# The first pass's SiLU written as h*(1+tanh(h/2))/2 in a fused attention and two-layer kernel

## The chip, the cores and the metric

One core of one Trainium2 chip runs the whole program in one launch. The metric is device time in microseconds. The kernel before took 858.95 us, the median of three runs (857.21 to 859.91).

## The reference

A linear attention with softmax over features (q) and over the sequence (k), then two feed-forward layers. The kernel's inputs are drawn so that q is spread by 0.8 and k by about 0.46; the weights are float64.

```
q_s = softmax(q, axis=-1);  k_s = softmax(k, axis=2)
kv  = einsum('bhsd,bhse->bhde', k_s, v);  x = einsum('bhsd,bhde->bhse', q_s, kv)
x   = x.transpose(0, 2, 1, 3).reshape(2304, 512)
h = x @ w_in1;  g = h * (1 / (1 + exp(-h)));      x = g @ w_out1     # SiLU, 512 -> 2048 -> 512
h = x @ w_in2;  g = h * tanh(log(1 + exp(h)));    out = g @ w_out2   # Mish, 512 -> 2048 -> 512
```

## The kernel before, in words

Every float32 product is made of three products of a reduced float32 type: an operand is split into a rounded high part and the rest, and high*high, high*low and low*high are added in the accumulator. So a step `x @ w` of 128 rows of w and 384 tokens takes three TensorE products.

The first layer runs in two passes over the hidden dimension, 8 of its 16 chunks of 128 each. The first pass (p = 0) goes through six blocks of 384 tokens, the second (p = 1) through five mostly 512 wide. For a block and chunk c, `ev_g1` makes h (12 products into one accumulator bank, 4 or 5 in turn), then SiLU, the rounded high part `g[:, 0]` and the rest `g[:, 1]`; `ev_g2` multiplies g into four accumulators (banks 0 to 3, 12 products), three chunks later (`SKEW = 3`, line 94). So at the start of a block four G1 stand in a row, and the third needs the bank of the first. At a block's end `ev_e` copies the four accumulators out, in the first pass with a plain copy, two on ScalarE and two on VectorE.

The first pass is interleaved with two other streams. The attention of the later blocks (`attn_steps`: k transposed with TensorE, its largest value on VectorE, Exp on ScalarE, back by TensorE and a ScalarE copy, the product with v, then q) works in banks 6 and 7, in the same queues. And in block 0 each weight tile is decoded from float64 just before its use (`w_decode`): on ScalarE one Prelu and one rounding copy, on VectorE a shift (`st`), a join (`wt`) and a subtraction (`wall`), 16 tiles in all.

Until the last part of the first pass the order of an engine's instructions is the choice of a scheduler: the program gives priorities (`at`) and the scheduler weighs them with its own idea of durations. From then on (`InOrder.on`) each engine's order is that of the code. In the profile an instruction of the scheduled part has line 57, one of the ordered part (and of the first attention block) line 59: the two calls of the recording helper. Once built, each engine works through its list in order, and an instruction that waits holds up all behind it.

The lines that matter: 712 takes the bank of h, 723 is SiLU from that bank, 724 the rounding (VectorE in the first pass, ScalarE in the second), 725 the subtraction, 747 and 749 the copies out of the accumulators. Where names follow, `gf` is the activation's result, `g` its two parts, `xs` the tokens, `knm` the largest value of k negated, `kz` its sum, `qmx` the largest value of q.

Of the kernel before, what the change touches and what calls it, by code (L numbers as in the profile page):

```python
# [10 lines left out]
ACTF = mybir.ActivationFunctionType  # L11
ALU = mybir.AluOpType
# [53 lines left out]
def attention_silu_mish(ctx: ExitStack, tc: tile.TileContext, q, k, v, w_in1, w_out1, w_in2, w_out2, out):  # L66
    nc = tc.nc
    V, S, G, T, SP = (InOrder(tc, e) for e in (nc.vector, nc.scalar, nc.gpsimd, nc.tensor, nc.sync))
# [69 lines left out]
    def banks(name, ids, n=1):  # L138
        i = turns[name] = (turns.get(name, -1) + 1) % len(ids)
        return psum[:, ids[i] * 512:(ids[i] + n) * 512]  # L140
# [99 lines left out]
    def w_get(kind, p, c):  # L240
        while p == 0 and (kind, p, c) not in wt:
            w_decode()
        return wt[(kind, p, c)]
# [465 lines left out]
    def ev_g1(p, j, c):  # L709
        w = w_get("G1", p, c)  # L710
        x = xs[(p, j)]
        h = banks("h1", (4, 5))[:, :blocks[p][j][1]]

        steps = [(kc, i) for i in range(3) for kc in range(KC)]
        if (p, j) == (0, 0) and c < 2:
            steps.sort()
        for n, (kc, i) in enumerate(steps):
            s = slice(kc * P, (kc + 1) * P)
            T.matmul(h, w[:, i // 2, s], x[:, kc, i % 2], start=(n == 0), stop=(n == len(steps) - 1))
        n = blocks[p][j][1]  # L720
        g = pools["g"].tile([P, 2, n], F32R, tag="g", name="g")
        gf = pools["gf"].tile([P, n], F32, tag="gf", name="gf")
        S.activation(out=gf, in_=h, func=ACTF.Silu)
        (S.copy if p else V.tensor_copy)(g[:, 0], gf)
        V.tensor_tensor(out=g[:, 1], in0=gf, in1=g[:, 0].bitcast(F32), op=ALU.subtract)
        gt[(p, j, c)] = g

# [12 lines left out]
    def ev_e(p, j):  # L740
        t0, n = blocks[p][j]
        for i, a in enumerate(acc[(p, j)]):
            y = xbT[:, i, t0:t0 + n]
            if p:
                V.tensor_tensor(out=y, in0=a[:, :n], in1=y, op=ALU.add)
            elif i % 2:
                V.tensor_copy(y, a[:, :n])
            else:
                S.copy(y, a[:, :n])

# [117 lines left out]
    def more():  # L870

        o_split()
        if not wait:
            return
        s, c, b = wait.pop(0)
        if s is None:
            ev_g2(1, len(WIDE) - 1, c)
            if c == NCH - 1:
                ev_e(1, len(WIDE) - 1)
            o_load(c - HALF - 3)  # L880
            return
        for n in range(BLK // P):
            second(s, c, b, n)
        if done[(s, b, 0)] == NCH:
            for n in range(BLK // P):
                out_tile(s, b, n)
        k = used[(s, c)] = used.get((s, c), 0) + 1
        if k == 2:
            o_load(s * NCH + c + O_RING)
# [3 lines left out]
    def pair(s, q):  # L893
# [64 lines left out]
        out=ident, in_=ident, compare_op=ALU.not_equal, fill=1.0, base=0, pattern=[[-1, P]], channel_multiplier=1  # L958
# [35 lines left out]
    for i, (what, p, j, c) in enumerate(events):  # L994
# [26 lines left out]
        if what == "E":  # L1021
            at(i if InOrder.on else i - X_LEAD)
            ev_e(p, j)
            continue
        (ev_g1 if what == "G1" else ev_g2)(p, j, c)
        if (what, p, j) == ("G1", 1, len(WIDE) - 1):
            n = c - HALF
# [72 lines left out]
```

## Time and the profile before

| | |
|---|---|
| median of three runs | 858.95 us |
| lowest and highest run | 857.21 and 859.91 us |
| span of the profiled execution, first to last instruction | 856.9 us |
| TensorE busy | 843.4 us, 98% |
| VectorE, ScalarE, GpSimd busy | 466.4, 365.3, 55.0 us |
| granted TensorE clock | 1.000 of full speed |

The profile lists no separate time of its execution beside the span; the median of the runs stands 2.05 us over that span. PE is TensorE's products and PEld its weight loads, which overlap; DVE is VectorE, ACT ScalarE, POOL GpSimd, SP the engine that issues DMAs. Busy times of neighbours on one engine overlap by some hundredths of a us, so what an instruction takes from its engine is the distance from its start to the next start.

### The profile page before, as it was taken

How to read it: one execution, taken by the hardware profiler on the slowest of the kernel's cores; microseconds unless marked ns; L12 is line 12 of the kernel's file. 1: busy time of each engine (PE TensorE's matmuls, PEld its weight loads, DVE VectorE, ACT ScalarE, POOL GpSimd, SP SyncE). 2: the span in 40 equal slices, each digit the busy share in tenths (PEclk: the TensorE clock that was granted, in tenths of full speed). 3: DMA queues.
4: the chain of work that ended last, by engine and by line, in shares of the span. 5: the costliest groups of instructions: out<-in, count | busy, mean ns of one | idle time of the engine just before them, and what ended most of it. 6: DMA issues, size and time to landing. Idle time of an engine off the chain costs nothing.

```text
span 856.9 us, 12318 instructions
## 1 busy us (share of the span) xinstructions
PE 843.4 (98%) x4666; PEld 755.6 (88%) x4666; DVE 466.4 (54%) x1004; ACT 365.3 (43%) x702; POOL 55.0 (6%) x82
## 2 busy tenths in 40 slices
PE   8899999999999999999999999999999999999998
PEld 7688988899999888898888899998999998999996
DVE  5998466673256656556574656675343554343431
ACT  5987254564244644335434444444322233322221
POOL 3145111221000000000000000000000000000000
PEclk9999999999999999999999999999999999999999
DMA  9996311220023438675633778888555455664312
GB/s 237 233 257 132 90 37 37 55 57 1 1 78 120 148 99 283 209 251 178 210 117 106 272 260 314 294 321 340 211 182 223 161 196 184 233 225 155 135 50 98
DMA packets 86105, 145.49 MB, mean 170 GB/s; under 512 B 33056, under 2 KB 60192, under 8 KB 82976
## 3 DMA queue, kind: packets, MB, share of 16 engines
q1 hardware_dynamic: 86048, 144.73, 52.2%
q8 instruction: 36, 0.59, 0.3%
q14 instruction: 21, 0.17, 0.1%
HBM read 105.38 MB, written 39.32 MB: 169 GB/s over the span
## 4 chain that ended last, share of the span: by engine, by line
PE 90%; DVE 3%; ACT 3%; DMA 2%; SPq 1%; issue 1%; ACTq 0%; DVEq 0%
PE psum L59 70%; PE psum L57 19%; DMA st<-in_moe_w_in_dram 2%; SPq L57 1%; ACT xa L57 1%; ACT wt L57 0%; DVE g L57 0%; DVE wt L59 0%; DVE kmx L57 0%; DVE wall L57 0%; DVE xs L59 0%; DVE wt L57 0%; ACT xs L59 0%; ACT L57 0%; ACT wall L57 0%
## 5 line engine op out<-in xcount | busy, mean ns | idle before, releaser
L59 PE MATMUL psum<-wall,g 128*128 128x512 f32 x864 | 210.1, 390 | 0.0
L59 PE MATMUL psum<-x,wall 128*128 128x384 f32 x1008 | 191.8, 338 | 0.0
L59 PEld LDWEIGHTS psum<-wall,g 128*128 128x128 f32 x864 | 161.3, 188 | 28.5 <-DVE xb L59 0.3
L59 PEld LDWEIGHTS psum<-x,wall 128*128 128x128 f32 x1008 | 179.9, 187 | 6.8
L59 PE MATMUL psum<-g,wall 128*128 128x512 f32 (+2 forms) x624 | 129.0, 360 | 0.0
L59 PE MATMUL psum<-xs,wall 128*128 128x512 f32 (+2 forms) x588 | 122.7, 362 | 0.2 <-ACT gf L59 0.2
L59 PEld LDWEIGHTS psum<-g,wall 128*128 128x128 f32 x624 | 109.0, 188 | 14.7
L59 PEld LDWEIGHTS psum<-xs,wall 128*128 128x128 f32 x588 | 102.7, 188 | 15.5 <-ACT gf L59 0.6
L59 DVE TENSOR_TENSOR hf<-psum,sc 128x384 f32<-128x384 f32 x72 | 40.0, 556 | 123.4 <-ACT sc L59 79.1
L57 PE MATMUL psum<-xs,wall 128*128 128x384 f32 x468 | 98.2, 349 | 3.2 <-ACT gf L57 2.3
L59 ACT COPY sc<-psum 128x384 f32<-128x384 f32 x72 | 34.5, 479 | 133.0 <-PE psum L59 133.0
L57 PEld LDWEIGHTS psum<-xs,wall 128*128 128x128 f32 x468 | 80.4, 189 | 7.5 <-ACT gf L57 3.6
L57 PE MATMUL psum<-g,wall 128*128 128x384 f32 x432 | 85.3, 343 | 0.5 <-DVE g L57 0.5
L57 PEld LDWEIGHTS psum<-g,wall 128*128 128x128 f32 x432 | 74.7, 188 | 2.1 <-DVE g L57 1.2
L59 ACT ACTIVATE hf<-hf 128x384 f32<-128x384 f32 x72 | 37.8, 525 | 84.9 <-DVE hf L59 84.8
L59 DVE TENSOR_TENSOR g<-gf,g 128x512 fp32r<-128x512 f32 (+2 forms) x49 | 30.5, 623 | 74.7 <-ACT g L59 74.4
L59 ACT ACTIVATE gf<-psum 128x512 f32<-128x512 f32 (+2 forms) x49 | 26.6, 543 | 98.6 <-PE psum L59 97.8
L59 DVE CAST g<-hf 128x384 fp32r<-128x384 f32 x96 | 34.5, 360 | 58.1 <-ACT hf L59 57.7
L59 DVE TENSOR_TENSOR g<-hf,g 128x384 fp32r<-128x384 f32 x96 | 53.6, 559 | 3.3
L59 ACT ACTIVATE wt<-st 128x512 f32<-128x512 f32 x48 | 32.0, 674 | 19.0 <-DMA st<-in_moe_w_out_dram 8.5
L57 DVE CAST g<-gf 128x384 fp32r<-128x384 f32 x39 | 16.1, 414 | 38.9 <-ACT gf L57 38.8
L57 ACT ACTIVATE gf<-psum 128x384 f32<-128x384 f32 x39 | 18.9, 491 | 40.9 <-PE psum L57 37.6
(123 smaller groups left out, 748.0 us busy)
## 6 DMA issues: line engine op xcount, KB each, us to landing
wall<-wq SPq DMA_DIRECT2D x16, 1792.0 KB, 7.5
st<-in_moe_w_in_dram SPq DMA_DIRECT2D x32, 512.0 KB, 4.8
st<-in_moe_w_out_dram SPq DMA_DIRECT2D x32, 512.0 KB, 4.4
wall<-wo SPq DMA_DIRECT2D x32, 512.0 KB, 3.6
wq<-wall SPq DMA_DIRECT2D x8, 1792.0 KB, 6.2
wo<-wall SPq DMA_DIRECT2D x16, 512.0 KB, 5.6
wqf<-wt SPq DMA_DIRECT2D x24, 256.0 KB, 3.3
wall<-wqf SPq DMA_DIRECT2D x24, 256.0 KB, 6.5
```

The costliest lines, as they stand in the source:

```text
L57: return call(*args, **kwargs)
L59: self.last = call(*args, **kwargs)
```

## The change

In the first pass SiLU becomes two instructions. ScalarE makes tanh(h/2) from the bank into `gf`; VectorE makes (gf + 1) * h, reading `gf` and the bank. The rounding copy goes from VectorE to ScalarE. What comes out is twice SiLU, and the half is put into the copy out of the accumulators. The second pass keeps Silu and its ScalarE rounding.

```
         gf = pools["gf"].tile([P, n], F32, tag="gf", name="gf")
-        S.activation(out=gf, in_=h, func=ACTF.Silu)
-        (S.copy if p else V.tensor_copy)(g[:, 0], gf)
+        if p:
+            S.activation(out=gf, in_=h, func=ACTF.Silu)
+        else:
+
+            S.activation(out=gf, in_=h, func=ACTF.Tanh, scale=0.5)
+            V.scalar_tensor_tensor(out=gf, in0=gf, scalar=1.0, in1=h, op0=ALU.add, op1=ALU.mult)
+        S.copy(g[:, 0], gf)
         V.tensor_tensor(out=g[:, 1], in0=gf, in1=g[:, 0].bitcast(F32), op=ALU.subtract)
...
             elif i % 2:
-                V.tensor_copy(y, a[:, :n])
+                V.tensor_scalar(out=y, in0=a[:, :n], scalar1=0.5, scalar2=None, op0=ALU.mult)
             else:
-                S.copy(y, a[:, :n])
+                S.mul(y, a[:, :n], 0.5)
```

The scheduler sees other instructions and makes another order on every engine. Three places in block 0 follow. ScalarE first, from the Prelu of the seventh weight tile; before, where `gf` is Silu's result and `kz` marks an Exp:

```order
L57 ACTIVATE wt_758<-st_709 128x512
L57 ACT_TABLE_LOAD
L57 ACTIVATE gf_429<-psum_126 128x384
L57 CAST wall_72<-wt_640 128x512
L57 CAST wall_72<-wt_703 128x512
L57 CAST wall_72<-wt_758 128x512
L57 ACTIVATE wt_818<-st_764 128x512
L57 ACTIVATE gf_506<-psum_126 128x384
L57 CAST wall_72<-wt_818 128x512
L57 ACT_TABLE_LOAD
L57 ACTIVATE xb_125,kz_459<-psum_126,knm_457 128x576
```

And now:

```order
L57 ACTIVATE wt_763<-st_713 128x512
L57 ACTIVATE gf_429<-psum_126 128x384
L57 ACTIVATE gf_507<-psum_126 128x384
L57 CAST wall_72<-wt_644 128x512
L57 CAST wall_72<-wt_707 128x512
L57 ACTIVATE wt_823<-st_769 128x512
L57 CAST wall_72<-wt_763 128x512
L57 CAST wall_72<-wt_823 128x512
L57 ACTIVATE xb_125,kz_460<-psum_126,knm_458 128x576
```

The table loads are gone here; in the whole program 23 of them become 3. Both chunks' activations now stand ahead of the roundings of the weights.

VectorE at the same place. Before, from the join of the seventh weight tile:

```order
L57 SCALAR_TENSOR_TENSOR wt_758<-wt_758,st_709 128x512
L57 CAST g_428<-gf_429 128x384
L57 TENSOR_TENSOR wall_72<-wt_640,wall_72 128x512
L57 TENSOR_TENSOR wall_72<-wt_703,wall_72 128x512
L57 TENSOR_TENSOR wall_72<-wt_758,wall_72 128x512
L57 SCALAR_TENSOR_TENSOR wt_818<-wt_818,st_764 128x512
L57 TENSOR_REDUCE knm_457<-psum_126 128x1
```

And now, from the shift of the eighth tile (`st_769`) to the join of the ninth (`wt_890`):

```order
L57 TENSOR_SCALAR st_769<-st_769 128x512
L57 TENSOR_TENSOR wall_72<-wt_644,wall_72 128x512
L57 TENSOR_TENSOR wall_72<-wt_707,wall_72 128x512
L57 SCALAR_TENSOR_TENSOR wt_763<-wt_763,st_713 128x512
L57 SCALAR_TENSOR_TENSOR wt_823<-wt_823,st_769 128x512
L57 TENSOR_REDUCE knm_458<-psum_126 128x1
...
L57 TENSOR_REDUCE qmx_468<-xb_125 96x4
L57 TENSOR_SCALAR st_829<-st_829 128x512
L57 SCALAR_TENSOR_TENSOR gf_429<-gf_429,psum_126 128x384
L57 SCALAR_TENSOR_TENSOR wt_890<-wt_890,st_829 128x512
L57 SCALAR_TENSOR_TENSOR gf_507<-gf_507,psum_126 128x384
L57 TENSOR_TENSOR g_428<-gf_429,g_428 128x384
```

What is left out there: two more subtractions of weights (`wall`), `kz`, the other `qmx` and the reciprocal `krz`, five rows in all. The multiplication that frees the first chunk's bank stands behind all of it.

TensorE, from the last four products of chunk 0's G1 on. Before:

```order
L57 MATMUL psum<-xs,wall 128x384 x19
L57 MATMUL psum<-ident,xa 128x96 x6
L57 MATMUL psum<-xs,wall 128x384 x21
L57 MATMUL psum<-g,wall 128x384 x8
L57 MATMUL psum<-ident,xa 128x96 x6
L57 MATMUL psum<-g,wall 128x384 x7
L57 MATMUL psum<-xs,wall 128x384 x12
L57 MATMUL psum<-g,wall 128x384
L57 MATMUL psum<-ident,xb 96x128 x6
L57 MATMUL psum<-g,wall 128x384 x10
L57 MATMUL psum<-xb,xa 64x64 x12
```

And now:

```order
L57 MATMUL psum<-xs,wall 128x384 x16
L57 MATMUL psum<-ident,xa 128x96 x6
L57 MATMUL psum<-xs,wall 128x384 x2
L57 MATMUL psum<-ident,xa 128x96 x6
L57 MATMUL psum<-xs,wall 128x384 x7
L57 MATMUL psum<-ident,xb 96x128 x6
L57 MATMUL psum<-xs,wall 128x384 x7
L57 MATMUL psum<-xb,xa 64x64 x12
L57 MATMUL psum<-xs,wall 128x384 x8
L57 MATMUL psum<-g,wall 128x384 x12
```

Ahead of these rows both lists have 8 of the 384-wide products on `xs`. `ident,xa` transposes k of a pair of heads, `ident,xb` takes its Exp back, and `xb,xa 64x64` is that pair's product with v. Before the first such product with v, G1 of chunk 4 and 26 products on `g` stood; now it stands amid G1 of chunk 3, with no product on `g` ahead of it.

## Rows read from the trace of the kernel before

**Rows 1.** The page, part 1: busy us, share of the span, instructions.

```profile
PE 843.4 (98%) x4666; PEld 755.6 (88%) x4666; DVE 466.4 (54%) x1004; ACT 365.3 (43%) x702; POOL 55.0 (6%) x82
```

**Rows 2.** Stretches: length, busy time by engine, clock, DMA share, GB/s.

```profile
20.00:60.00 40.00, 35.65 (x269) 29.19 (x270) 38.01 (x88) 36.27 (x66) 11.49 (x13) 1.00 1.03 251
60.00:90.00 30.00, 29.60 (x214) 26.50 (x214) 25.93 (x66) 23.09 (x46) 14.70 (x19) 1.00 0.80 160
90.00:250.00 160.00, 158.96 (x1049) 148.30 (x1048) 81.89 (x202) 70.65 (x132) 21.91 (x33) 1.00 0.12 31
250.00:800.00 550.00, 549.83 (x2751) 490.50 (x2750) 294.29 (x591) 213.63 (x419) 0.00 (x0) 1.00 0.61 212
```

**Rows 3.** Groups by line and shape: busy us, mean ns of one, idle before.

```profile
L57 ACT ACT_TABLE_LOAD x22 | 28.2, 1283 | 4.0 <-PE psum L57 2.3 <-PEq L1084 0.7 <-DVE knm L57 0.6
...
L57 ACT ACTIVATE gf<-psum 128x384 f32<-128x384 f32 x39 | 18.9, 491 | 40.9 <-PE psum L57 37.6 <-DVE g L57 1.6 <-issue 1.6
...
L59 DVE TENSOR_TENSOR hf<-psum,sc 128x384 f32<-128x384 f32 x72 | 40.0, 556 | 123.4 <-ACT sc L59 79.1 <-PE psum L59 44.4
...
L57 DVE TENSOR_TENSOR g<-gf,g 128x384 fp32r<-128x384 f32 x39 | 24.5, 628 | 0.9
...
L57 DVE CAST g<-gf 128x384 fp32r<-128x384 f32 x39 | 16.1, 414 | 38.9 <-ACT gf L57 38.8
...
L57 ACT CAST xs<-xa 128x384 fp32r<-128x384 f32 x16 | 7.4, 511 | 4.6 <-PE psum L57 4.4
...
L57 DVE COPY xb<-psum 128x384 f32<-128x384 f32 x8 | 4.1, 552 | 7.5 <-PE psum L57 7.5
...
L57 ACT COPY xb<-psum 128x384 f32<-128x384 f32 x8 | 3.4, 481 | 10.1 <-PE psum L57 10.1
```

**Rows 4.** TensorE in order of time: start, us, what, idle before and releaser.

```profile
33.83 0.79 PE L57 MATMUL psum<-xs,wall 128*128 128x384 f32 x3 [1.41 <-ACT gf L57]
...
40.59 0.98 PE L57 MATMUL psum<-g,wall 128*128 128x384 f32 x4 [0.49 <-DVE g L57]
...
48.19 0.92 PE L57 MATMUL psum<-xb,xa 96*64 96x64 f32 x24
...
52.11 1.68 PE L57 MATMUL psum<-xs,wall 128*128 128x384 f32 x8 [0.89 <-ACT gf L57]
...
91.44 2.24 PE L57 MATMUL psum<-g,wall 128*128 128x384 f32 x12
93.52 2.24 PE L57 MATMUL psum<-xs,wall 128*128 128x384 f32 x12
```

**Rows 5.** VectorE in order of time, 34 to 40 us.

```profile
34.00 0.43 DVE L57 TENSOR_SCALAR st<-st 128x512 uint32<-128x512 uint32 x1 [0.85 <-DMA st<-in_moe_w_in_dram]
34.34 0.68 DVE L57 SCALAR_TENSOR_TENSOR wt<-wt,st 128x512 uint32<-128x512 uint32 x1
...
35.21 1.89 DVE L57 TENSOR_TENSOR wall<-wt,wall 128x512 fp32r<-128x512 f32 x3
...
37.62 0.75 DVE L57 TENSOR_REDUCE knm<-psum 128x1 f32<-128x576 f32 x1
...
39.00 0.74 DVE L57 TENSOR_REDUCE qmx<-xb 96x4 f32<-96x256 f32 x2
```

**Rows 6.** ScalarE in order of time, 31 to 48 us.

```profile
31.99 1.28 ACT L57 ACT_TABLE_LOAD   x1
33.28 0.49 ACT L57 ACTIVATE gf<-psum 128x384 f32<-128x384 f32 x1
...
39.67 0.74 ACT L57 ACTIVATE xb<-psum,knm 128x576 f32<-128x576 f32 x1
40.31 0.19 ACT L57 ACTIVATION_READ_ACCUMULATOR xb<-psum,knm 128x1 f32 x1
...
45.99 1.34 ACT L57 ACTIVATE xb<-xb 96x256 f32<-96x256 f32 x4
47.23 0.79 ACT L57 COPY xa<-psum 96x768 f32<-96x768 f32 x1
```

## The prediction, on record before the changed kernel ran

> **What bounds the kernel now.** I read the page's engine shares first: TensorE is busy for 843.4 of 856.9 us [rows 1], so a change can save at most what TensorE still idles, and every new idle us of TensorE is paid in full unless an old one goes with it. Then the stretches [rows 2], to see where it idles: 4.35 us from 20 to 60 us (40.00 less 35.65), 0.40 from 60 to 90, 1.04 from 90 to 250, and 0.17 in the 550 us after that. The first pass begins within the first stretch, and there VectorE (38.01 of 40 us) and ScalarE (36.27) are nearly full as well, with the decoding of 16 weight tiles, the attention and the first chunks. Last the order of time in that stretch. The reader is to see that two of TensorE's gaps end with ScalarE's SiLU: 1.41 us before 33.83 and 0.89 us before 52.11 [rows 4]. In front of the first stands a table load of 1.28 us [rows 6].
>
> **What the change removes.** ScalarE has 22 table loads in the scheduled part at 1283 ns [rows 3]; 23 become 3 in the whole program, since Exp and Tanh no longer alternate with another table. That is 20 x 1.283 = 25.7 us of ScalarE. It is worth to the end only what TensorE waits for, the two gaps: 2.30 us. All others lie beside a busy TensorE.
>
> The Trainium skill ("ScalarE: Activation LUTs", section on table sets) puts exp and tanh into one set, asks to batch activations by set, and counts about 2.66 us for a switch with a drain. Here the activation starts 1.29 us after its load does [rows 6], so I see the load and no drain; the page would make it 53 us of ScalarE where the rows make it 25.7. Neither is time at the end by itself; what it could free is the first rival below.
>
> **What it adds.** Per chunk, 48 times: on ScalarE a rounding of 0.51 us (a 128x384 rounding, nearest row `xs`), 24.5 us in all, so ScalarE's sum hardly changes. On VectorE a multiplication in place of a rounding of 0.41. The trace shows no 384-wide multiplication of this form; the nearest are the addition of a bank and a tile, 0.556, and the subtraction of `g`, 0.628 [rows 3]. I take 0.56, reading a bank and a tile as this does, and keep 0.63. That is +0.15 to +0.21 us a chunk, 7 to 10 us of VectorE beside a busy TensorE, except where VectorE decides. The scaled copies out stand for 0.55 and 0.48 us [rows 3] and I leave them at that: an activation from a bank of this size takes 0.49, so twelve on ScalarE could cost 0.01 each, and they lie three chunks ahead of the next use of their banks.
>
> **What it moves: the bank.** Before, h's bank was free when ScalarE had read it. Now it is free when VectorE has multiplied. In steady running G1 of chunk c+2 starts three groups of 12 products after G1 of chunk c, that is 3 x 2.08 = 6.2 us (12 products start 2.08 us apart [rows 4], 0.1733 each), and activation and multiplication take 0.49 + 0.56 and two handovers: no stop. At a block's start four G1 stand in a row and 2.08 us are left for the same 1.05 and handovers: still enough if VectorE is free. In block 0 it is not free, and the new order shows it.
>
> **The stop, step by step.** The activations of chunks 0 and 1 come early, about 32 and 32.5 us, as no load stands before them. But VectorE's list has the multiplication of chunk 0 behind thirteen instructions, of which the first is the shift at 34.00. That one waits for its DMA [rows 5], as it will again. From there, start to start: shift 0.34; two weight subtractions and two joins at 0.60 (the three subtractions of rows 5 take 1.89), 2.40; largest of k 0.67; two more subtractions 1.20; `kz`, `qmx`, `krz`, `qmx` 0.10 + 0.33 + 0.10 + 0.33 (two `qmx` take 0.74); shift 0.34. Sum 5.81, so the multiplication starts at 39.81 and ends at 40.37. Does anything on the way wait longer? The Exp that `kz` waits for starts when `knm` ends, about 37.5, and takes 0.74 + 0.19 [rows 6]: 38.4, while `kz` is due at 38.6. No. So G1 of chunk 2 starts at about 40.4 where it started at 33.83 [rows 4]. TensorE has only the transposes of k between, and stands for about 5 us.
>
> What is lost is not all of that, since the attention chain comes earlier. I count at a place that both lists have, the first pair's product with v, at 48.19 before [rows 4]. Now: from 39.81 two multiplications with a join between and one subtraction of `g` (0.47 + 0.60 + 0.47 + 0.47), two `qmx` 0.66, `knm` of the next pair 0.75: 43.23. Then Exp 0.64 to the next start, four Exp of q 1.34, the copy back 0.79 [rows 6]: 46.0. TensorE waits for this too, and starts at 46.05, 2.14 us earlier than before. By then it has issued 1 + 7 + 16 + 2 + 7 + 7 = 40 wide products, before 8 + 19 + 21 + 12 on `xs` and 8 + 7 + 1 + 10 on `g`, 86. The 46 that are missing take 46 x 0.1733 = 7.97 us; less 2.14, TensorE is 5.83 us behind.
>
> From there TensorE has work ready (g of chunks 0 and 1 are done while it catches up with G1 of chunk 3), so it only loses its old gaps: the 0.89 before 52.11 goes, since chunk 5's bank will be free long before, and I let the 0.40 idle from 60 to 90 us go with it, as the attention steps come earlier against TensorE. 5.83 - 0.89 - 0.40 = 4.54. The 1.41 gap needs no term: it lies before the count. The 1.04 us from 90 to 250 end with attention steps and I leave them.
>
> **The sum.** +4.5 us on the span, 856.9 to about 861.4. The median of the runs stands 2.05 us above the span, and I carry that over: 858.95 + 4.5 = 863.5 us. For this case alone I expect 861.5 to 866: if all idle after the count comes back (0.89 + 0.40 + 1.04 and some 0.5 of small gaps) +3.0, and with a multiplication of 0.63 and the small gaps of new handovers +6, give or take a us between runs. A measurement of this kernel tells about 0.3%, 2.6 us, from no change.
>
> **Rivals.**
> Faster: the loads' wake was what held TensorE in block 0. Then 1.41 and 0.89 go: 856.65, which alone is within 0.3%; and if all idle from 20 to 60 us goes, 4.35, 854.6. For it: ScalarE is 91% busy there and both gaps end with SiLU. Against it: the multiplication's place in VectorE's list, which this case would have to pass over. It decides if the multiplication of chunk 0 ends before about 35 us. The rule on table sets of the Trainium skill ("ScalarE: Activation LUTs") leads here.
>
> No change: block 0 is bound by the decoding on VectorE, not by TensorE, and TensorE's lost 5.8 us are found again when the weights would have stopped it. VectorE pays 8 x 0.15 = 1.2 us, the two gaps give back 2.3: 857.9. For it: VectorE is 95% busy from 20 to 60. Against it: TensorE was 89% busy in that stretch and full behind it, so there are no later stops of that size to lose.
>
> Slower still: the same stop comes again at the starts of the later blocks, where VectorE also copies two accumulators out (2 x 0.55) and splits tokens. Five starts at up to 1 us: 863.5 + 5 = 868.5. Against it: before 90 us VectorE is at 86%, after it at 51% [rows 2], and the 2.08 us hold the 1.05 and one copy pair.
>
> That the change doesn't do what it says is excluded for the loads: the new list has three.
>
> **How the numbers follow.** My case 0.64, slower still 0.08, no change 0.17, faster 0.11. Each but the last two is slower by over 0.3%: 0.72; within, 0.17; faster by over 0.3%, 0.11. The range is 858.5 to 868.5: above it half of the slower-still case, below it the faster case and a part of no change, 2 in 10 in all.
>
> **What would show it.** In the changed profile: a TensorE gap of about 5 us that ends near 40 us with VectorE's `gf`; the first product with v near 46 us; TensorE's idle time from 20 to 60 us about 8 us instead of 4.35 and unchanged from 90 on; three table loads; 48 multiplications of 0.56 to 0.63 us. I am wrong if G1 of chunk 2 starts before 36 us, if the stop is there but the product with v also comes 6 us earlier, or if TensorE's idle time from 90 to 250 us grows by more than 1 us.

## The result, and the profile after

| | before | after |
|---|---|---|
| median of four runs | 858.52 us | 867.18 us |
| lowest and highest | 857.21 and 859.91 us | 867.10 and 869.06 us |
| span of the profiled execution | 856.9 us | 865.2 us |
| mean granted clock | 1.000 | 0.994 |

The ratio is 1.0108, 95% interval 1.0086 to 1.0130: slower by about 9 us. The forecast was 863.5 us, 861.5 to 866 for my own case, with 868.5 as the upper end of the whole range. The direction and the stop in block 0 came as told, the size did not: the span grew by 8.3 us where I had 4.5, and the time lies above the range of my own case.

The page of the changed kernel, part 1, to set beside [rows 1]:

```profile
PE 843.9 (98%) x4666; PEld 756.8 (87%) x4666; DVE 470.9 (54%) x1004; ACT 361.8 (42%) x730; POOL 51.4 (6%) x82
```

TensorE's work is the same, so all of the 8.3 us is time in which it stood or ran slowly. The stretches, as in [rows 2]:

```profile
20.00:60.00 40.00, 32.05 (x236) 27.13 (x236) 38.17 (x87) 31.87 (x65) 9.25 (x13) 0.87 1.04 257
60.00:90.00 30.00, 28.74 (x225) 26.00 (x222) 23.98 (x63) 17.09 (x42) 12.60 (x18) 1.00 0.66 153
90.00:250.00 160.00, 157.65 (x1042) 146.56 (x1041) 82.86 (x196) 67.77 (x145) 22.59 (x35) 1.00 0.12 31
250.00:800.00 550.00, 548.58 (x2743) 488.79 (x2742) 295.64 (x591) 221.20 (x433) 0.00 (x0) 1.00 0.59 209
```

TensorE's idle time, the length less its busy time, grew in every one: 4.35 to 7.95, 0.40 to 1.26, 1.04 to 2.35, 0.17 to 1.42 us. ScalarE has been relieved (31.87 for 36.27 us in the first stretch), and TensorE still lost. In the first stretch the granted clock, TensorE's share of full speed, is 0.87, where it was 1.00.

The groups by line and shape, as in [rows 3]:

```profile
L57 DVE TENSOR_TENSOR g<-gf,g 128x384 fp32r<-128x384 f32 x39 | 22.0, 563 | 10.6 <-ACT g L57 10.6
L57 DVE SCALAR_TENSOR_TENSOR gf<-gf,psum 128x384 f32<-128x384 f32 x39 | 21.3, 547 | 32.3 <-ACT gf L57 32.2
L57 ACT CAST g<-gf 128x384 fp32r<-128x384 f32 x39 | 19.9, 511 | 15.2 <-DVE gf L57 15.0
...
L57 DVE TENSOR_SCALAR xb<-psum 128x384 f32<-128x384 f32 x8 | 4.1, 550 | 7.9 <-PE psum L57 7.9
L57 ACT ACTIVATE xb<-psum 128x384 f32<-128x384 f32 x8 | 3.5, 489 | 9.0 <-PE psum L57 9.0
...
L59 ACT ACT_TABLE_LOAD x2 | 2.6, 1283 | 0.0
```

The durations that I had taken from neighbouring rows came true but for one: the multiplication takes 0.547 us (0.56 taken), the rounding 0.511, the scaled copies 0.550 and 0.489; the subtraction of `g`, which I had kept at 0.63, takes 0.563. What is new is the last column: ScalarE stands 15.0 us at the rounding until VectorE has multiplied.

TensorE in order of time, as in [rows 4]:

```profile
33.92 0.71 PE L57 MATMUL psum<-ident,xa 96*128 96x96 f32 x6 [1.95 <-DMA xa<-in_k_dram]
39.70 1.01 PE L57 MATMUL psum<-xs,wall 128*128 128x384 f32 x2 [5.07 <-DVE gf L57]
...
41.38 2.59 PE L57 MATMUL psum<-xs,wall 128*128 128x384 f32 x7
43.76 1.48 PE L57 MATMUL psum<-ident,xb 128*96 128x128 f32 x6
...
46.41 0.92 PE L57 MATMUL psum<-xb,xa 96*64 96x64 f32 x24
...
287.00 5.64 PE L59 MATMUL psum<-xs,wall 128*128 128x512 f32 x24
293.58 5.76 PE L59 MATMUL psum<-xs,wall 128*128 128x512 f32 x24 [0.93 <-ACT gf L59]
```

The stop that the prediction worked out is there: 5.07 us, ended by VectorE's `gf` at 39.70, and the first product with v at 46.41 (46.05 worked out). Behind it the reader should see that the seven products at 41.38 take 0.34 us each and not 0.17. VectorE over the stop, as in [rows 5], and ScalarE's two activations, as in [rows 6]:

```profile
33.07 0.43 DVE L57 TENSOR_SCALAR st<-st 128x512 uint32<-128x512 uint32 x1 [0.34 <-DMA st<-in_moe_w_in_dram]
...
39.11 0.54 DVE L57 SCALAR_TENSOR_TENSOR gf<-gf,psum 128x384 f32<-128x384 f32 x1
```

```profile
31.17 0.54 ACT L57 ACTIVATE gf<-psum 128x384 f32<-128x384 f32 x1
32.01 0.49 ACT L57 ACTIVATE gf<-psum 128x384 f32<-128x384 f32 x1 [0.31 <-PE psum L57]
```

Chunk 0's tanh ends at 31.71, and its multiplication starts at 39.11: 7.4 us in VectorE's list.

**Where the time went.** I count at two places that all lists have: the first 48 products on `g` without a break behind the attention (200.64 us before), and the second pass's first product on `g` (291.00 us before). From the second on to the end at most 0.6 us more is lost in any kernel, and up to 0.3 is won back in two. The last column is the part of the one before it that is lost between the second pass's first G1 (280.07 us before) and the second place; what is left of it is lost at block 5's start, the last of the first pass. Positive is later than before. One profiled execution each:

| kernel | median us | ratio, 95% interval | at the first place | from there to the second | of that, in the second pass |
|---|---|---|---|---|---|
| after | 867.18 | 1.0086 to 1.0130 | +6.30 | +1.87 | +1.24 |
| early | 866.34 | 1.0062 to 1.0104 | +3.61 | +1.84 | +1.20 |
| hold | 866.49 | 1.0066 to 1.0103 | +3.96 | +1.85 | +1.22 |
| preload | 867.59 | 1.0078 to 1.0111 | +6.63 | +1.88 | +1.24 |
| from1 | 863.10 | 1.0033 to 1.0061 | +1.23 | +1.83 | +1.19 |
| preload2 | 866.74 | 1.0068 to 1.0108 | +10.10 | +0.60 | -0.01 |
| round_dve | 866.79 | 1.0074 to 1.0109 | +5.89 | +0.80 | +0.28 |
| early_rv_pre | 863.89 | 1.0037 to 1.0074 | +3.56 | +0.49 | -0.01 |
| round_act | 861.14 | 1.0014 to 1.0035 | +2.08 | +0.02 | -0.01 |
| tanh_only | 865.30 | 1.0039 to 1.0081 | +1.90 | +0.02 | +0.01 |
| nobank | 864.10 | 1.0051 to 1.0078 | +3.33 | +1.20 | +1.19 |
| from1_rv_pre | 859.69 | 1.0004 to 1.0025 | +0.45 | +0.48 | -0.01 |
| swap | 857.52 | 0.9983 to 1.0006 | -1.70 | +0.02 | +0.01 |

One of from1_rv_pre's twelve runs took 1813.37 us, for a reason that the record does not show; without it the median is 859.61. The other runs of one kernel spread by 1.4 to 5.7 us, and a profile shows one of them: of preload2 the longest, of early, hold, round_dve and swap the shortest, of tanh_only the second shortest. So medians and profiles are both needed. The losses behind the first place repeat to 0.05 us between kernels that share what causes them (1.83 to 1.88), those up to it do not: after, preload and preload2 have the same lists there and lose 6.30, 6.63 and 10.10.

### The profile page after: what moved, and what is told of

Read it like the earlier page. It is cut to its first block, busy times and chain, and to the rows that moved or that the text cites. A ratio compares the mean times of both kernels' runs of the same rounds, so it can differ in the third digit from the quotient of the medians.

```text
span 865.2 us, 12361 instructions
## 1 busy us (share of the span) xinstructions
PE 843.9 (98%) x4666; PEld 756.8 (87%) x4666; DVE 470.9 (54%) x1004; ACT 361.8 (42%) x730; POOL 51.4 (6%) x82
## 4 chain that ended last, share of the span: by engine, by line
PE 86%; DVE 5%; ACT 3%; DMA 3%; issue 1%; SPq 1%; POOL 1%; ACTq 0%; POOLq 0%; DVEq 0%
PE psum L59 67%; PE psum L57 18%; DMA st<-in_moe_w_in_dram 2%; SPq L57 1%; DVE kmx L57 1%; DVE wt L59 1%; DMA st<-in_moe_w_out_dram 1%; DVE xs L59 1%; ACT xa L57 1%; ACT xs L59 1%; ACT wt L59 0%; DVE xs L57 0%; DVE qz L57 0%; DMA qt<-in_q_dram 0%; POOL qn L57 0%
## 5 line engine op out<-in xcount | busy, mean ns | idle before, releaser
L57 DVE SCALAR_TENSOR_TENSOR gf<-gf,psum 128x384 f32<-128x384 f32 x39 | 21.3, 547 | 32.3 <-ACT gf L57 32.2
L59 DVE SCALAR_TENSOR_TENSOR wt<-wt,st 128x512 uint32<-128x512 uint32 x48 | 33.0, 687 | 1.4
```

The lines of the kernel that those rows point to most:

```text
L57: return call(*args, **kwargs)
L59: self.last = call(*args, **kwargs)
```

## The experiments

### hold: TensorE kept busy through the stop

```
-            T.transpose(o, kt[:, r].rearrange("p h d -> p (h d)"), ident[:KP, :KP])
+            last = T.transpose(o, kt[:, r].rearrange("p h d -> p (h d)"), ident[:KP, :KP])
+        if not first["acc"] and not first.get("held"):
+            first["held"] = True
+            with tc.issue_after(last.ins):
+                for _ in range(19):
+                    T.matmul(psum[:, 3 * 512:3 * 512 + P], ident, ident, start=True, stop=True)
```

> The changed kernel with 19 products of the unit matrix on TensorE behind the first transposes of k of the scheduled part, that is in its stop before chunk 2; they write an accumulator bank that is not in use yet and nothing reads them. Theory: they keep the granted clock at 1.0, where it fell to 0.5 from about 35 to 45 us; the attention chain on the other engines decides most of that stretch, so full speed is worth about 0.9 us: 866.3 (865.7 to 866.8). Rival: the half clock's 5.4 us of products cost half of their time, 2.7 us: 864.5. If the clock falls nevertheless, or costs nothing: 867.2.

The clock no longer falls. The granted clock is the third number from the end of a row; here from 36 to 38 and from 42 to 44 us, of after and then of hold:

```profile
36.00:38.00 2.00, 0.00 (x0) 0.00 (x0) 2.00 (x5) 1.38 (x3) 0.00 (x0) 0.50 1.30 161
42.00:44.00 2.00, 2.00 (x9) 1.84 (x8) 1.97 (x5) 1.40 (x5) 0.82 (x2) 0.50 1.03 378
```

```profile
36.00:38.00 2.00, 2.00 (x20) 2.00 (x20) 2.00 (x5) 1.35 (x3) 0.00 (x0) 1.00 1.27 200
42.00:44.00 2.00, 2.00 (x16) 1.97 (x15) 1.97 (x7) 2.00 (x7) 0.99 (x1) 1.00 1.05 365
```

```profile
34.45 4.43 PE L57 MATMUL psum<-ident 128*128 128x128 f32 x38
39.36 1.14 PE L57 MATMUL psum<-xs,wall 128*128 128x384 f32 x5 [0.48 <-DVE gf L57]
```

The 19 products (two rows each in the trace) fill the stop. G1 of chunk 2 starts at 39.36, hardly earlier than in after (39.70), but the rest of block 0 runs at full clock: 6.30 becomes 3.96. The medians differ by 0.7 us, as expected and within their spread. The profile is of hold's shortest run and of one of after's middle runs, and the mean clock is 0.998 to 1.000 in all six runs of hold and 0.994 to 0.996 in the four of after. So the clock's fall is part of block 0's loss; its worth is 0.7 us by the medians and 2.3 us in these two executions, which is likely too much.

### early: the multiplication ahead in VectorE's list

```
+            tc.cur_priority -= 9000
             V.scalar_tensor_tensor(out=gf, in0=gf, scalar=1.0, in1=h, op0=ALU.add, op1=ALU.mult)
+            tc.cur_priority += 9000
```

> The changed kernel with one thing moved: the multiplication (tanh+1)*h of the first pass is given an earlier priority, so the scheduler puts chunk 0's and chunk 1's multiplications right behind their tanh in VectorE's list (both now stand ahead of the shift of the seventh weight tile). Theory: the 5 us stop of TensorE before chunk 2, and the half clock behind it, are due to that place alone. Then TensorE has no gap over 1.5 us between 30 and 45 us, the granted clock stays at 1.0, and the time falls by about 5 us from 867.2 to 862 (860.5 to 863.5); the 3.3 us that come later stay. Rival: VectorE's added work and the longer path to g delay block 0 anyway, and what is not lost in one stop is lost in many: 866 or more.

```profile
33.76 0.96 PE L57 MATMUL psum<-xs,wall 128*128 128x384 f32 x4 [0.93 <-DVE gf L57]
35.59 0.72 PE L57 MATMUL psum<-ident,xa 96*128 96x96 f32 x6 [0.86 <-DMA xa<-in_k_dram]
...
41.80 0.69 PE L57 MATMUL psum<-ident,xa 96*128 96x96 f32 x6 [1.28 <-DMA xa<-in_k_dram]
```

The stop is gone and the clock stays at 1.00, and 3.61 us are still lost. Smaller gaps have come, two of them before transposes of k that wait for their DMA. The median, 866.34, is the rival's and not the 862 expected. The profile is of the shortest run; of the six only two have a mean clock of 1.000, the others 0.995 to 0.997. So to take this stop away by another order does not take the loss away.

### from1: block 0 as before, the change from block 1 on

Against the changed kernel:

```
-        if p:
+        if p or j == 0:
             S.activation(out=gf, in_=h, func=ACTF.Silu)
...
-        S.copy(g[:, 0], gf)
+        (V.tensor_copy if (p, j) == (0, 0) else S.copy)(g[:, 0], gf)
```

The copies out of block 0 are not halved here.

> The tanh form for blocks 1 to 5 of the first pass; block 0 as in the kernel before (Silu on ScalarE, rounding on VectorE, copies out without the half). 11 table loads instead of 3 (23 before). Theory: block 0's stop is 5 of the 8.3 us, and the loads that come back stand in block 0 as before: 862.2 (861 to 863.5), with what is lost after 90 us unchanged. Rival: the loss is spread over all blocks, so leaving out one of six saves about 1.4 us: 865.8.

TensorE's gaps in block 0 are those of before again (1.26 and 0.89 us ended by SiLU, at 33.83 and 52.24), and 3.4 us of span are lost all the same, at 1.23 + 1.83 of the two places. The median is 863.10, for 862.2 expected. So the 8.3 us split into some 5 us of block 0 and some 3 us behind it, of which the prediction had nothing.

### preload and preload2: the last table load moved

```
+        if (p, j) == (1, 0):                      # preload2: behind the roundings of the tokens
+            S.activation(out=warm, in_=mask[:, 0, :1], func=ACTF.Silu)
```

In preload the same line stands behind the last tanh.

> The changed kernel with one more ScalarE instruction: a Silu of one column behind the last tanh of the first pass, so that the table of the second pass is loaded there, in the ordered part, some 5 us before the second pass's first Silu. Theory: the first Silu of the second pass waits for a load of 1.28 us that was on TensorE's path (its gap of 0.93 us before 293.58): 867.2 - 1.2 = 866.0, and that gap gone. Rival: the gap comes from the copies and weight work ahead of that Silu on ScalarE, and the load lies beside it: 867.2 and a gap of 0.5 us or more at the same place.

> The changed kernel, with a one-column Silu on ScalarE at the end of the first pass's last but four copy step (where ScalarE stood idle for 2.21 us in the changed kernel's profile), so that the last table load stands before the second pass's first bank instead of behind it. Theory (that load is what the second pass's first wait is made of): the loss of 1.24 us between 287 and 299 us goes, the gap of 0.93 us that ends with ScalarE's gf there too, and the total is 867.2 - 1.2 = 866.0 us. Rival (ScalarE's list is late there for what stands before the load, so that the load only takes the place of a wait): the deficit at the second pass's third chunk stays at 8.1 to 8.3 us and the total at 867.2.

ScalarE at the second pass's start, of after, of preload, and of preload2:

```profile
281.61 2.16 ACT L59 CAST xs<-xa 128x512 fp32r<-128x512 f32 x4
285.98 0.62 ACT L59 CAST wall<-wt 128x512 fp32r<-128x512 f32 x1 [2.21 <-DVE wt L59]
...
291.63 1.28 ACT L59 ACT_TABLE_LOAD   x1
292.93 0.60 ACT L59 ACTIVATE gf<-psum 128x512 f32<-128x512 f32 x1
```

```profile
280.92 1.28 ACT L59 ACT_TABLE_LOAD   x1
...
283.40 2.17 ACT L59 CAST xs<-xa 128x512 fp32r<-128x512 f32 x4
287.78 0.62 ACT L59 CAST wall<-wt 128x512 fp32r<-128x512 f32 x1 [2.20 <-DVE wt L59]
```

```profile
285.36 2.17 ACT L59 CAST xs<-xa 128x512 fp32r<-128x512 f32 x4
287.55 1.28 ACT L59 ACT_TABLE_LOAD   x1
...
289.73 0.62 ACT L59 CAST wall<-wt 128x512 fp32r<-128x512 f32 x1 [0.69 <-DVE wt L59]
```

In preload the load stands ahead of the tokens' roundings, delays them, and VectorE's weights with them: the idle 2.20 us stay, and so does the loss (+1.88). In preload2 the load lies in that idle time, and the loss falls from 1.87 to 0.60, about the 1.24 expected: all that was lost in the second pass. So the load costs this where it stands, and it matters whose work stands behind the place to which it goes. It does so only because ScalarE's list is late there already. The second pass's first Silu starts 3.34 us after its first G1 in the kernel before, 5.93 in after and 4.49 in preload2. In round_dve (below) the load stays in front of that Silu, but ScalarE no longer waits at the first pass's roundings; there it starts after 4.94 us, and 0.28 us are lost:

```profile
290.12 1.28 ACT L59 ACT_TABLE_LOAD   x1
291.42 0.60 ACT L59 ACTIVATE gf<-psum 128x512 f32<-128x512 f32 x1
```

preload2's median moved by 0.4 us only, for 1.2 expected; block 0 varies by more. In preload2's own profile it cost 3.8 us more than in after's:

```profile
40.41 0.43 DVE L57 TENSOR_SCALAR st<-st 128x512 uint32<-128x512 uint32 x1 [1.54 <-DMA st<-in_moe_w_out_dram]
40.75 0.55 DVE L57 SCALAR_TENSOR_TENSOR gf<-gf,psum 128x384 f32<-128x384 f32 x1
```

The same list as after's, but a second shift ahead of the multiplication waits for its DMA: the bank is free 1.6 us later, and the stop is 6.62 us long.

### round_dve and round_act: who rounds

```
-        S.copy(g[:, 0], gf)
+        (S.copy if p else V.tensor_copy)(g[:, 0], gf)      # round_dve, against after
```

```
-        (S.copy if p else V.tensor_copy)(g[:, 0], gf)
+        S.copy(g[:, 0], gf)                                # round_act, against before
```

> The changed kernel, with the first pass's rounding given back to VectorE, so that ScalarE does not wait for VectorE's multiplication before it rounds. Block 0's list keeps the same stop. Theory (the loss behind block 0 is ScalarE's list standing at the rounding until VectorE has multiplied, with attention steps and weights queued behind it): of the 8.3 us some 4.9 stay (block 0), and the 1.4 up to 207 us and 0.63 at 258 us go, 1.24 at the second pass's start at least in part: 867.2 - 2.0 to 3.3 = 863.9 to 865.2 us. Rival (the loss behind block 0 is the bank held until VectorE has multiplied, whoever rounds): 867.2 within 0.6 us, or more, as VectorE has 48 more instructions of 0.41 us.

> The kernel before with one part of the change alone: the first pass's rounding on ScalarE instead of VectorE; Silu, its 23 table loads and the plain copies stay. Here ScalarE rounds its own result and waits for nobody. Theory (the loss behind block 0 comes from the back and forth with VectorE, not from 24.5 us more of ScalarE): behind 90 us TensorE loses under 0.5 us against before; in block 0, where ScalarE is 91% busy, eight roundings of 0.51 us are 4.1 us more, of which I expect 1 to 4 to reach the end: 860 to 863 us. Rival (ScalarE's added work alone makes the loss behind block 0): 2 us or more are lost between 90 and 290 us as well, 863 to 866 us.

Who waits for whom on ScalarE from 90 to 290 us in after (total, times, longest):

```profile
ACT g L57 <- DVE gf L57: 12.9, 21, 1.2
...
ACT g L59 <- DVE gf L59: 9.1, 9, 1.8
```

In neither of the two other kernels do these rows exist. round_act, with 24.5 us more of ScalarE's roundings and all 23 loads, loses 2.1 us up to the first place, and nothing behind it; its median, 861.14, is as expected. So it is not ScalarE's added work. Taking the wait away (round_dve) brings 1.87 to 0.80, nearly all of it in the second pass (1.24 to 0.28), and TensorE's idle time from 90 to 250 us from 2.35 to 1.52, though VectorE has 48 instructions more. So the wait at the rounding, with what stands behind it in ScalarE's list, is a cause. It is not the only one: at block 5's start 0.52 us are still lost, and in tanh_only (below), which has no multiplication to wait for, the idle time from 90 to 250 us is 1.94 for 1.04 before, so a part of that growth belongs to the new order. The total of round_dve fell by 0.4 us, not by the 2 to 3.3 expected, so of the total the expectation missed. The stop of block 0 stayed (5.3 us), with the idle time from 20 to 90 us 1.0 longer in this execution.

### early_rv_pre and from1_rv_pre: the three mends together, with and without block 0

Both have VectorE round in the first pass and the load at preload2's place; the first has early's priority besides, the second keeps Silu in block 0.

> Three edits of the changed kernel together: the multiplication put ahead in VectorE's list, the first pass's rounding back on VectorE, the Silu table loaded at the end of the first pass. Theory (stop in block 0, ScalarE's wait at the rounding, and the table load account for all 8.3 us but 0.8 that the early order kept at the first product with v): 858.7 + 0.8 = 859.5 us, at most 861. Rival (the bank held until VectorE multiplies costs 3 us behind block 0 whatever the order): 858.7 + 0.8 + 3 = 862.5 us or more.

> The change in blocks 1 to 5 alone (block 0 keeps Silu and its loads), rounding on VectorE in the first pass, Silu's table loaded at the end of the first pass. Theory (block 0's list, ScalarE's wait at the rounding and the table load are all of the loss): 858.9 + 0.5 to 1.5, that is 859.4 to 860.4 us, against 863.1 with rounding on ScalarE and the load where it was. Rival (the bank held until VectorE multiplies costs 3 us behind block 0, whoever rounds): 862 to 863.5 us.

from1_rv_pre came as the theory had it: 859.69 us, 0.45 and 0.48 lost at the two places. So behind block 0 the two edits together take away all of the 3.1 us but some 0.9; 0.49 of these lie at block 5's start. Of the kernels whose SiLU goes by tanh and multiplication it is the best, and it is no better than before (1.0004 to 1.0025).

early_rv_pre missed: 863.89 where 859.5 to 861 were expected. With no stop of 5 us, no clock fall (1.00 from 32 to 50 us) and no wait at the rounding, 3.56 us are lost by the first place, against 0.45 with block 0 as before. So this order of block 0 loses some 3.1 us without the stop. It is not the changed kernel's order, so this is no share of what that one loses.

### nobank, tanh_only, swap: the bank, the gain alone, and the order

```
-            V.scalar_tensor_tensor(out=gf, in0=gf, scalar=1.0, in1=h, op0=ALU.add, op1=ALU.mult)
+            V.scalar_tensor_tensor(out=gf, in0=gf, scalar=1.0, in1=gf, op0=ALU.add, op1=ALU.mult)   # nobank
```

tanh_only is round_dve without that line. swap is the kernel before, and the lists are finished before the function is exchanged. What comes out of these three is not SiLU.

```
-        S.activation(out=gf, in_=h, func=ACTF.Silu)
+        a = S.activation(out=gf, in_=h, func=ACTF.Silu); SWAP.update(() if p else [a.ins.name])
...
         attention_silu_mish(tc, *args)
+    for f in nc.m.functions:
+        for b in f.blocks:
+            b.instructions = [i.__replace__(func=ACTF.Tanh) if i.name in SWAP else i for i in b.instructions]
```

> The changed kernel, but its multiplication reads gf twice, not gf and h's bank (so what comes out is not SiLU): same instructions, same engines, rounding on ScalarE, and the bank is free at the end of the tanh. Theory (block 0's 4.9 us are the bank held behind VectorE's list; behind block 0 ScalarE still stands at the rounding until VectorE has multiplied): no TensorE gap of 5 us that ends with VectorE's gf near 40 us, total 858.9 + 2 to 3.5 = 861 to 862.5 us. Rival (VectorE's added work and the later g cost it, not the bank): 865 us or more.

> The gain alone: the first pass has ScalarE's tanh in Silu's place and no multiplication, the rounding stays on VectorE and the copies out are scaled; three table loads instead of 23. The SiLU itself is left out (g is the two parts of tanh(h/2)), so that h's bank is free when ScalarE has read it, as before. Theory (the loads are worth the two gaps of 1.41 and 0.89 us and no more): 858.9 - 2.3 = 856.6 us, between 855.5 and 858. Rival 1 (what the loads held is all that TensorE idles from 20 to 60 us): 854.6. Rival 2 (the new list on VectorE loses in block 0 what the loads gave): 859 or more.

> The loads' worth with nothing moved: the kernel before, scheduled with Silu, so that every engine's list is that of before; then, in the finished lists, the first pass's Silu is exchanged for tanh, which leaves out 20 table loads and the SiLU itself (what comes out is the two parts of tanh(h)). Theory (the loads are worth TensorE's gaps of 1.41 and 0.89 us, and what was lost without them in the kernel with tanh and no multiplication came from the other list): 858.5 - 2.3 = 856.2 us, between 855.2 and 857.2, and no gap of 2.4 us near 40 us that ends with VectorE's g. Rival 1 (all idle time from 20 to 60 us is the loads'): 854.2. Rival 2 (without the loads the attention or the decoding stops TensorE in the same places): 858 or more.

nobank took 864.10 us, between theory and rival. The gap by `gf` is gone: G1 of chunk 2 follows chunk 1's, but for the transposes of k, and chunk 3's ends near 37.4. Then TensorE stops for `g` instead:

```profile
40.42 1.01 PE L57 MATMUL psum<-g,wall 128*128 128x384 f32 x2 [3.06 <-ACT g L57]
```

The bank was the nearest wait, and `g` of chunk 0, made by the same late place in VectorE's list, is the next. Freeing it brings 6.30 to 3.33 at the first place, in one execution each. At block 5's start the bank is all. There after has a gap that ends with the multiplication:

```profile
257.63 4.58 PE L59 MATMUL psum<-xs,wall 128*128 128x384 f32 x24 [0.21 <-DVE gf L59]
```

In nobank it has none, and the 0.63 us lost there (1.87 less 1.24 in the table) become 0.01.

tanh_only is the surprise. But for the factor in the copies out it only takes away: 20 loads. It should have gained 2.3 us, and it took 865.30. TensorE, and the end of VectorE's list ahead of `g`:

```profile
40.31 1.62 PE L57 MATMUL psum<-g,wall 128*128 128x384 f32 x4 [2.44 <-DVE g L57]
...
76.85 0.92 PE L57 MATMUL psum<-xb,xa 96*64 96x64 f32 x24 [1.54 <-ACT xa L57]
```

```profile
34.09 0.43 DVE L57 TENSOR_SCALAR st<-st 128x512 uint32<-128x512 uint32 x1 [1.11 <-DMA st<-in_moe_w_in_dram]
...
39.48 0.41 DVE L57 TENSOR_SCALAR st<-st 128x512 uint32<-128x512 uint32 x1
39.82 0.35 DVE L57 CAST g<-gf 128x384 fp32r<-128x384 f32 x1
```

The rounding of chunk 0 stands where after has the multiplication, behind the same thirteen instructions; before it stood at 34.95, right behind the join. So the late place comes from the scheduler's new order and needs no multiplication. In swap, with tanh and three loads but the order of before, both of SiLU's gaps are gone, and the products on `g` start at 40.21 (40.59 before):

```profile
33.45 0.72 PE L57 MATMUL psum<-ident,xa 96*128 96x96 f32 x6 [0.72 <-DMA xa<-in_k_dram]
33.95 4.28 PE L57 MATMUL psum<-xs,wall 128*128 128x384 f32 x21
...
40.21 0.98 PE L57 MATMUL psum<-g,wall 128*128 128x384 f32 x4 [1.29 <-DVE g L57]
...
58.85 0.38 PE L57 MATMUL psum<-ident,qn 96*128 96x96 f32 x2 [1.04 <-POOL qn L57]
```

swap is 1.70 us ahead of before at the first place in its profile, and 0.7 us in the median (857.52 against 858.25, not told from no change), where 855.2 to 857.2 us were expected; the profile is of its shortest run. Of the 2.3 us, longer waits for VectorE's `g` (0.49 before, 1.29 now) and GpSimd's `qn` (1.04) take a part back. Between swap and tanh_only lie the order of the instructions and the factors, the 0.5 inside the tanh and the one in the copies out, which come first at a block's end: 3.60 us at the first place, 7.8 us in the medians. So the order that the scheduler makes without the loads costs more than the loads did.

## Why the prediction was right, and where its size was off

- **The stop, step by step.** Right, to 0.7 us: multiplication at 39.11 (39.81), G1 of chunk 2 at 39.70 (40.4), first product with v at 46.41 (46.05). The last of these agrees partly by luck: no term had the clock's fall, and where the clock stayed up (hold) that product came at 44.94. Until then 46 products of 0.1733 us were missing, as counted; less 1.78 us, TensorE was 6.19 us behind, for 5.83.
- **What comes back.** I let 0.89 and 0.40 us return, for +4.54. Block 0 cost 5.1 (6.30 less the 1.23 that from1 loses without it), so 1.1 us came back for 1.29. The size was right, but not for the whole reason: the clock's fall is in it, with 0.7 us by the medians and 2.3 in one pair of executions (hold), and the sum had no term for it. And without this stop block 0 is not free: with the bank freed 3.33 us are lost up to the first place (nobank), in another order 3.61 and 3.56 (early, early_rv_pre).
- **"Unchanged from 90 on."** This is the step that failed. I had written that 6.2 us in steady running, and 2.08 at a block's start, hold activation, multiplication and handovers of 1.05 us and a bit, and asked about the bank alone. The runs show 3.1 us that no term of the sum had, in three parts. At block 5's start 0.63 us are lost, and that is the bank: 2.08 us were not enough there (0.01 left in nobank, 0.52 in round_dve). In the second pass 1.24 us are lost, and that is ScalarE's list: the rounding waits for VectorE, what stands behind it waits with it, and a table load comes on top; 0.28 are left without the wait, nothing with the load elsewhere. Up to the first place 1.23 us are lost (from1), of which the wait is a part (0.45 in from1_rv_pre, one execution each) and the new order, by tanh_only's idle time, another. My own sign of being wrong, over 1 us more idle time from 90 to 250 us, came true at 1.31.
- **The remaining loads.** I counted 20 loads away and never asked where the three stand that stay. One stands right in front of the second pass's first Silu, and the 1.24 us above go when it moves into an idle time of ScalarE (preload2).
- **The loads' worth.** Sized right as a sum of gaps (2.3), but with the order kept only 1.7 us came in the profile and 0.7 in the median, and with the new order it was a loss (tanh_only).
- **Slower still, 868.5.** Its mechanism, the stop again at later block starts, was real at one place, 0.63 us at block 5 and not up to 1 us at each of five. The time came near this rival by the other losses. It lies above the 861.5 to 866 of my own case, and only this rival had widened the range to hold it: that it does is luck.
- **Faster; no change.** Both fell. The multiplication of chunk 0 ended at 39.65 and not before 35 us; with it put ahead (early) the time is still 866, and TensorE's lost time was not found again in the decoding.

Left open: how the 5.1 us of block 0 divide among stop, clock and order; which places make the 3.1 us that another order loses without the stop (early_rv_pre has gaps of 0.46 to 1.67 us there, ended by k's DMA, the Exp `xb` and GpSimd's `qn`), and how much of the medians' 7.8 us between swap and tanh_only is the clock.

## What to carry to other kernels

Where a scheduler orders the work, an edit that removes something it counts, such as table loads, is first of all a new order, and here that order cost more than the loads did: price the order, by exchanging the function in the finished lists if need be, before pricing the instructions. An instruction that waits for another engine also holds up what is queued behind it: look in each list at what stands behind each new handover. And of what is left over, ask where it stands: here one load in front of a waited-for bank cost 1.24 us in a list that was late already, and 0.28 in one that was less so.

## What the hardware showed

The granted clock fell from 2.4 to 1.2 GHz (0.50) after TensorE had stood 1.95 us, worked 0.71 and stood on in the 5.07 us stop; it was back at 1.00 by 46 us, after TensorE had worked from 39.70 on without a gap. In tanh_only it fell behind a stop of 2.44 us: 0.51 from 40 to 42 us. In early, with gaps of 0.93, 0.86 and 1.28 us, it stayed at 1.00 in the profile. Yet in round_act it was 0.79 from 50 to 52 us and 0.50 from 52 to 54, where the gaps before were of 0.34 and 1.12 us, so the length of one stop does not tell it. In tanh_only the runs part by it: the two with a mean clock of 0.998 and 1.000 took 861.38 and 860.28 us, the four from 0.993 to 0.995 took 865.26 to 865.97. Only the first has a profile, so whether the clock alone makes these 4 to 5 us, or a longer stop that also made it fall, isn't shown. The multiplication that reads a bank and a tile took 0.547 us, a tanh 0.490 against Silu's 0.491, and a copy out with a factor 0.489 on ScalarE against 0.481 without.
